# Low-part second products of the first layer one step later, other order at block ends, a third h buffer

## The chip, the cores and the metric

The kernel runs on one core of a Trainium2 chip. A core has five engines that run side by side, each through its own queue in order: TensorE (PE) multiplies, ScalarE (ACT), VectorE (DVE) and GpSimd (POOL) work on tiles, SyncE (SP) issues transfers. The metric is the time of one execution in microseconds (us) as the device counts it; lower is better.

## The reference, cut

```python
X = np.fft.fft(np.fft.fft(x, axis=1), axis=2).real      # x: 2 x 3008 x 256
x = X.reshape(6016, 256)
h = x @ w_in1;  r = maximum(h, 0);  x = (r * r) @ w_out1     # first layer, hidden width 2048
h = x @ w_in2;  out = (h - tanh(h)) @ w_out2                 # second layer
```

## The kernel before

**Precision.** Each operand of a product is split in a high and a low part, and a product is three matmuls: high by high, low by high, high by low. A matmul here takes a stationary block of 128 x 128 weights and streams 376 or 378 columns.

**Staging.** The transform over the sequence is folded into eight blocks of output frequencies (two batches by four classes). The first layer works through (block, f) pairs, f being one of 16 slices of 128 of the hidden layer; STEPS lists them, 128 steps in all. Block 0 runs its first four slices, then block 1 runs whole, then block 0 the rest; from step 32 on the blocks follow one another. The second layer starts when the last block of the first is done.

**One step of the first layer** has five parts, which the loop at L808 calls for different steps in one iteration i:
- `front(i + 2)`, six matmuls (L352, tile w<-uv,wt): the first products, into two PSUM banks. The four banks of `w` hold two steps.
- `back(i)`, twelve matmuls (L517): the second products into four accumulators a00 to a11 (half of the model dimension m, half of the columns s). Eight take gh, the high part of the squared values, and four take gl, the low part.
- `mid(i + 2)`: DVE makes pb (L490) and the two halves of h (L491, L492) from the banks; ACT takes the positive part (L493), squares it into gh (L494) and again into h (L495).
- `late(i + 1)`: POOL (DVE in the first eight slices of block 0) makes gl = h - gh (L504).
- background: conversions, folds and splits of weights for later stages. From step 48 on it is `make_w2` (L543), two of its parts per iteration; they stand on DVE at L227, L229, L231 (conversion from float64), L558 (low part) and L566 to L575 (sums), on ACT at L219, L556 and L573. `tc.issue_after(last_mid[0].ins)` holds them behind the mid of their iteration on DVE.

**Buffers.** gh and gl have three buffers, h has two (L454): DVE may write h of step k at L491 only when POOL has read h of step k - 2 at L504.

**Block ends.** After the last slice of a block (and after slice 3 of block 0) `evac` copies the four accumulators out: ACT those of m = 0, DVE those of m = 1 (L531). The next block's first `back` writes the same four banks; between the two lies one `front`. At three places the transforms of later blocks use the accumulators first (DFT, L822).

**What sets the order.** The engines run in the order in which the scheduler leaves the instructions, which follows the code except where it finds a later one ready sooner. In the last block `restore(f)` loads the second layer's weights over slice f's.

Of the kernel before, what the change touches and what calls it, by code (L numbers as in the profile page):

```python
# [21 lines left out]
# Rows of the sequence that share one folded row n, as (sign, offset): row = offset + sign * n.  # L22
# First two of a half against the last two (their mirror rows).
# [5 lines left out]
# Folded rows n in the order of their partitions, -1 for none: the even ones in the first tile and  # L29
# a half, the odd ones in the rest.  # L30
# [3 lines left out]
# Columns d and 256 - d side by side (0 goes with 128).  # L34
COLS = np.array([list(range(128)), [128] + [256 - d for d in range(1, 128)]])
# Classes of output frequencies k; S - k comes with k.
# [11 lines left out]
# Transforms of later blocks, at the start of a block of the first layer.  # L48
HALF = 4
DFT = {(0, HALF): (2, 3), (3, 0): (4,), (5, 0): (6, 7)}  # L50
# The first block waits with its second half while the weights that it takes are made.
STEPS = [(0, f) for f in range(HALF)] + [(1, f) for f in range(NF)]
STEPS += [(0, f) for f in range(HALF, NF)] + [(blk, f) for blk in range(2, NBLK) for f in range(NF)]
# The steps that make the weights of the first layer.
# [4 lines left out]
def x_layout(x):  # L59
    """Per row tile, the two terms of the sums that the folds begin with: (sums of pieces 0 and 2,  # L60
    of pieces 1 and 3), each for both halves of the columns. The column 0 goes with 128 in sums of
    its own."""
    out = np.zeros((B, 3, 2, 128, 2, 2, 2, 128), x.dtype)
    used = ROWS >= 0
    for g in range(2):
        r = np.zeros((2, 4, B, 384, 128), x.dtype)
        for s, (sg, of) in enumerate(PIECES[g]):
            rows = (of + sg * ROWS[used]) % S
            for h in range(2):
                r[h, s, :, used] = x[:, rows][:, :, COLS[h]].swapaxes(0, 1)  # L70
        r = r.reshape(2, 4, B, 3, 128, 128)
        for s in range(2):
            for i in range(2):
                for term, h in ((0, i), (1, 1 - i)):
                    out[:, :, term, :, i, s, g] = r[h, s + 2 * term]
                    out[:, :, term, :, i, s, g, 0] = r[(i + s) % 2, s + 2 * term, ..., 0]
    return out.reshape(B, 3, 2, 128, 1024)
# [13 lines left out]
def tables():  # L91
    n = ROWS
    w = np.where(n < 0, 0.0, 1.0)
    w[(n == 0) | (n == NROW - 1)] = 0.5
    res = []
    for c, k in enumerate(KS[:3]):
        a = 2 * np.pi * ((k[None, :] * n[:, None]) % S) / S
        first = np.cos(a) * w[:, None]
        if c < 2:
            second = np.sin(a) * w[:, None]  # L100
        else:
            a2 = 2 * np.pi * ((k[None, :] * (752 - n)[:, None]) % S) / S
            second = np.cos(a2) * w[:, None]
        t = np.concatenate([first.reshape(3, 128, -1), second.reshape(3, 128, -1)])
        if c == 0:
            t[:, :, NROW] = 0.0
        # [row tile, 128, (first hi, first lo, second hi, second lo), N]
        t = np.stack(_split(t)).reshape(2, 2, 3, 128, -1).transpose(2, 3, 1, 0, 4)
        res.append(np.ascontiguousarray(t.reshape(3, 128, 4, -1)))
    return res  # L110
# [28 lines left out]
def spectral_mlps(  # L139
# [25 lines left out]
    def psw():  # L165
        """Two banks; as one tile in the first block."""
# [11 lines left out]
    def ring(name):  # L178
        """A tile of the ring that holds tables and inputs of the second layer."""
# [34 lines left out]
    # float64, as pairs of words, to float32: the exponent's bias is changed by a product in the  # L214
    # words' own reading as float32; what is under float32's range comes out as tiny.
# [5 lines left out]
    def conv(layer, f):  # L221
        """Yields after each part."""
        r = raw.pop((layer, f))
        lo, hi = r[:, :, 0], r[:, :, 1]
        y = main.tile([128, 512], I32, tag="cy", name="cy")
# [14 lines left out]
    def transform_in(f, p):  # L240
        """A slice of w1_in under the transform over the model dimension: rows for the even and
        odd parts."""
# [14 lines left out]
    def clear_middle(f):  # L257
        """The middle frequency's row of the odd part, which only the whole products take."""
# [4 lines left out]
    def middle_load(f):  # L263
        """The middle frequency's row of the odd part as a column, in its two parts."""
# [26 lines left out]
    def fold(b, t):  # L291
        """The folded rows for odd k, split in two, and those for even k. Yields after each step."""
# [38 lines left out]
    def split_even(b, t):  # L331
        """Splits the folded rows for even k, in the place of those for odd k."""
# [24 lines left out]
    def dft_mm(blk):  # L357
        """Folded transform over the sequence for one class of even k: even and odd parts."""
# [19 lines left out]
    def dft_pair(blk, t):  # L378
        """Folded transform over the sequence for the classes of odd k, from row tile t: even and
        odd parts, of even rows and of odd rows. The second class has the difference of the two."""  # L380
# [29 lines left out]
    def dft_evac(blk):  # L410
        """The parts split in two, and the middle frequency's row of the even part in all
        partitions."""
# [8 lines left out]
    def pair_evac(blk):  # L421
        """The same for the classes of odd k. Yields after the first class."""
# [30 lines left out]
    def tiles():  # L453
        h = main.tile([128, 2, NM], F32, tag="h", name="h", bufs=2)  # L454
# [25 lines left out]
    def mid(blk, f):  # L480
        n = NC[BLOCKS[blk][1]]
        p = wps.pop((blk, f))
        h, gh, gl = tiles()
        if blk == 0 and f in WHOLE:
            for s in range(2):
                act.activation(h[:, s, :n], bank(p, s)[:, :n], AF.Relu)
        else:
# [4 lines left out]
            last_mid[0] = dve.tensor_tensor(h[:, 1, :n], pb[:, :n], bank(p, 1)[:, :n], ALU.subtract)  # L492
            act.activation(h[:, :, :n], h[:, :, :n], AF.Relu)  # L493
# [12 lines left out]
    def back(blk, f):  # L506
        n = NC[BLOCKS[blk][1]]
        if f == 0 or blk == 0 and f in FIRST:
            acc[1, blk] = [psa(0), psa(1)]
        w = wt[f]  # L510
        first = f == 0 or blk == 0 and f in FIRST
        last = f == NF - 1 or blk == 0 and f in LAST
        gh, gl = gt.pop((1, blk, f))
        for g, wi in ((gh, 2), (gh, 3), (gl, 2)):
            for m in range(2):
                for s in range(2):
                    pe.matmul(  # L517
                        acc[1, blk][m][s][:, :n],
                        w[:, wi, m * 128:(m + 1) * 128],
                        g[:, s, :n],  # L520
                        start=(first and g is gh and wi == 2),
                        stop=(last and g is gl),
                    )

# [14 lines left out]
    # Pairs of slices in seven products: the blocks of w_in are (slice, half of the model  # L539
    # dimension), those of x are (half of the model dimension, half of the columns).  # L540
    sums, x7 = {}, {}

    def make_w2():  # L543
        """The second layer's weights split in two, and the sums of the blocks of w_in."""
# [3 lines left out]
        for f in range(NF):  # L548
# [15 lines left out]
            y = main.tile([128, 512], F32, tag="cy", name="sums")  # L564
# [14 lines left out]
    def load_sums(j):  # L579
        """Gives the parts of the four sums, hi and lo."""  # L580
# [11 lines left out]
    def make_x7(blk):  # L592
        """The blocks of x that are operands as they are, and the sums, split in two."""
# [28 lines left out]
    def pair(blk, j, back, prev, extra):  # L622
        """The products of a pair, with the last pair's second products between them, and what
        comes after the products. Gives the blocks that are not done."""
# [13 lines left out]
        def block(i, k, c, d=None):  # L638
            """Block (slice, half of the columns) of the product, and what comes after it."""
# [24 lines left out]
        step(p21, 1)  # tanh  # L664
        step(c11, 1)  # add
        step(back, 2)
        step(p12, 1)  # copy
        step(p21, 1)  # sub
        step(c11, 2)  # tanh, sub
# [3 lines left out]
        step(p12)  # gl  # L673
        step(c11, 1)  # copy
        step(p21, 1)  # copy
        step(c11)  # gl
        step(p21)  # gl
# [4 lines left out]
        step(c22, 1)  # add  # L682
        step(back, 3)
        step(c22, 2)  # tanh, sub
        product(p, s4, x["b22"], False)
        step(c12, 2)  # tanh
        step(c22, 1)  # copy
        step(c12, 1)  # sub
        step(back)
        product(z, a[3], x["t4"], False)  # L690
        step(c21, 1)  # add
        step(c22)  # gl
        return c12, c21

    def back_pair(blk, j):
        """Yields after each half of a block."""
# [32 lines left out]
    def weights1(f, p):  # L729
        """Converted values of slice f to the operands of its products."""  # L730
# [9 lines left out]
    # so that ScalarE has its functions before it needs them  # L740
# [58 lines left out]
    # tables of later blocks  # L799
# [8 lines left out]
    for i in range(-2, NS - 2):  # L808
# [11 lines left out]
        # transforms of later blocks, while the accumulators are free  # L820
        if (blk, f) in DFT:
# [10 lines left out]
            look(i + 3)  # L832
        if i >= 0:
            back(blk, f)
        if f == NF - 1 or blk == 0 and f in LAST:
            evac(blk, blk == 0 and f == NF - 1)
        mid(*STEPS[i + 2])
        if i >= -1:
            late(*STEPS[i + 1])
        # weights of later steps  # L840
# [16 lines left out]
        # the rest of the folds and the second layer's weights  # L857
# [10 lines left out]
        if blk == NBLK - 1:  # L868
            restore(f)
# [6 lines left out]
        # tables  # L876
# [4 lines left out]
    # the second layer  # L881
    def back_last():
        for f in (NF - 2, NF - 1):
            back(NBLK - 1, f)
            restore(f)
            if f == NF - 1:
                evac(NBLK - 1)
# [23 lines left out]
def w_layout(w_in, w_out):  # L911
    """Per slice of the hidden layer, rows of w_in and of w_out, as the words of the numbers."""
# [22 lines left out]
```

## Time and profile before

| | us |
|---|---|
| Three runs, median (lowest to highest) | 1032.24 (1032.15 to 1033.52) |
| Profiled execution, span from first to last instruction | 1030.0 |
| PE busy | 970.4 (94%) |
| DVE busy | 806.7 (78%) |
| ACT busy | 731.0 (71%) |
| POOL busy | 245.9 (24%) |

The profile is of one execution and gives its span alone; the median of the runs lies 2.2 us above it, and 2.2 us is taken as what lies around the span. A share is a mean over the whole span. A matmul's end is modelled, and it overlaps the next one, so a busy PE is not yet a PE at its best pace. "Idle before" an instruction is time in which its engine had nothing running, with the event that ended it.

### The profile page before, as it was taken

The numbers are of one execution on the slowest core, as the hardware profiler recorded it, in microseconds if no ns is written. First come the engines' busy times: TensorE is split into PE (matmuls) and PEld (weight loads), VectorE is DVE, ScalarE is ACT, GpSimd is POOL, SyncE is SP. The second block draws the span as 40 slices with busy tenths as digits, with TensorE's granted clock in tenths as the row PEclk, the third lists the DMA queues.
The fourth block names the chain that finished last, engine by engine and source line by source line (L and its number), as shares of the span: only waits on it lengthen the run. The fifth ranks groups of instructions, "written<-read, shape, count | busy, mean of one in ns | idle before, by whom it ended". The sixth has DMA issues, their size and how long they took to land.

```text
span 1030.0 us, 15447 instructions
## 1 busy us (share of the span) xinstructions
PE 970.4 (94%) x5542; PEld 948.3 (92%) x5542; DVE 806.7 (78%) x1483; ACT 731.0 (71%) x1289; POOL 245.9 (24%) x171
## 2 busy tenths in 40 slices
PE   4988898999898899898999999999999999999998
PEld 3877897999888898788999999999999999999998
DVE  6999779657898878989567877968778787876776
ACT  2877767787777867877876766767667676766665
POOL 1145515653445435545530000000000000000000
PEclk9999999999999999999999999999999999999999
DMA  8666140206222313514740000101001010000000
GB/s 306 208 202 159 30 142 21 31 1 252 102 94 101 136 70 121 183 62 151 270 160 1 31 31 1 61 1 53 9 1 61 1 61 1 2 31 1 31 1 31
DMA packets 36332, 82.66 MB, mean 80 GB/s; under 512 B 7328, under 2 KB 21152, under 8 KB 36256
## 3 DMA queue, kind: packets, MB, share of 16 engines
q1 hardware_dynamic: 35280, 79.34, 22.0%
q0 software_dynamic: 976, 2.34, 1.4%
q8 instruction: 43, 0.70, 0.3%
q14 instruction: 33, 0.27, 0.1%
HBM read 55.97 MB, written 25.69 MB: 79 GB/s over the span
## 4 chain that ended last, share of the span: by engine, by line
PE 68%; DVE 11%; POOL 4%; ACT 3%; issue 3%; DMA 0%; POOLq 0%; DVEq 0%; ACTq 0%
PE a L352 28%; PE w L352 28%; PE a L517 12%; POOL gl L504 4%; DVE h L491 2%; DVE h L492 2%; ACT h L495 1%; DVE pb L490 1%; ACT gh L494 1%; DVE val L231 1%; DVE val L229 1%; DVE cy L227 1%; DVE sums L569 1%; DVE sums L571 1%; DVE sums L575 0%
## 5 line engine op out<-in xcount | busy, mean ns | idle before, releaser
L504 POOL TENSOR_TENSOR gl<-h,gh 128x752 fp32r<-128x752 f32 (+1 forms) x120 | 224.2, 1868 | 224.0 <-ACT h L495 174.3
L352 PE MATMUL a<-gh,wt 128*128 128x376 f32 (+1 forms) x1024 | 259.6, 335 | 0.0
L517 PE MATMUL a<-gh,wt 128*128 128x376 f32 (+1 forms) x1024 | 205.4, 340 | 6.4 <-DVE y L531 2.4
L517 PEld LDWEIGHTS a<-gh,wt 128*128 128x128 f32 x1024 | 179.8, 190 | 11.8 <-DVE y L531 4.7
L352 PEld LDWEIGHTS a<-gh,wt 128*128 128x128 f32 x1024 | 184.5, 188 | 0.0
L352 PE MATMUL a<-gl,wt 128*128 128x376 f32 (+1 forms) x512 | 171.8, 335 | 0.0
L352 PE MATMUL w<-x,sums 128*128 128x376 f32 (+1 forms) x768 | 163.4, 334 | 0.0
L493 ACT ACTIVATE h<-h 128x752 f32<-128x752 f32 (+1 forms) x125 | 104.1, 832 | 76.9 <-DVE h L492 74.3
L352 PE MATMUL w<-uv,wt 128*128 128x376 f32 (+1 forms) x777 | 156.9, 337 | 0.7 <-POOL wt L259 0.7
L653 DVE TENSOR_TENSOR gl<-h,gh 128x376 fp32r<-128x376 f32 (+1 forms) x256 | 138.8, 546 | 11.3 <-ACT gh L651 10.6
L651 ACT CAST gh<-h 128x376 fp32r<-128x376 f32 (+1 forms) x256 | 129.3, 507 | 17.1 <-DVE h L649 16.8
L517 PE MATMUL a<-gl,wt 128*128 128x376 f32 (+1 forms) x512 | 113.3, 343 | 27.7 <-POOL gl L504 27.7
L352 PEld LDWEIGHTS w<-uv,wt 128*128 128x128 f32 x777 | 136.8, 190 | 1.2 <-POOL wt L259 1.0
L647 ACT ACTIVATE tanh<-h 128x376 f32<-128x376 f32 (+1 forms) x192 | 99.8, 520 | 52.8 <-DVE h L643 47.5
L649 DVE TENSOR_TENSOR h<-h,tanh 128x376 f32<-128x376 f32 (+1 forms) x192 | 106.6, 555 | 37.6 <-ACT tanh L647 31.3
L352 PEld LDWEIGHTS w<-x,sums 128*128 128x128 f32 x768 | 135.4, 188 | 0.2 <-ACT u L681 0.2
L517 PEld LDWEIGHTS a<-gl,wt 128*128 128x128 f32 x512 | 88.8, 190 | 37.3 <-POOL gl L504 37.0
L494 ACT ACTIVATE gh<-h 128x752 fp32r<-128x752 f32 (+1 forms) x128 | 106.9, 835 | 3.0
L495 ACT ACTIVATE h<-h 128x752 f32<-128x752 f32 (+1 forms) x128 | 106.7, 833 | 3.0
L490 DVE SCALAR_TENSOR_TENSOR pb<-ub,w,w 128x376 f32<-128x376 f32 (+1 forms) x125 | 74.9, 600 | 40.0 <-PE w L352 37.4
L643 DVE TENSOR_TENSOR h<-u,w 128x376 f32<-128x376 f32 (+1 forms) x128 | 69.6, 543 | 39.1 <-ACT u L681 39.1
L491 DVE TENSOR_TENSOR h<-w,pb 128x376 f32<-128x376 f32 (+1 forms) x125 | 68.5, 548 | 40.0 <-POOL gl L504 29.6
(98 smaller groups left out, 1129.7 us busy)
## 6 DMA issues: line engine op xcount, KB each, us to landing
stage<-w SPq DMA_DIRECT2D x32, 512.0 KB, 3.7
tab<-tab SPq DMA_DIRECT2D x12, 752.0 KB, 7.8
w2s<-w SPq DMA_DIRECT2D x16, 512.0 KB, 2.6
wt<-w2s SPq DMA_DIRECT2D x16, 512.0 KB, 3.6
sums<-sums SPq DMA_DIRECT2D x15, 512.0 KB, 3.5
tab<-tab SPq DMA_DIRECT2D x6, 756.0 KB, 5.6
x<-y SPq DMA_DIRECT2D x12, 376.0 KB, 3.1
x2f<-x SPq DMA_DIRECT2D x6, 752.0 KB, 4.6
```

What stands on the lines that cost most here:

```text
L352: pe.matmul(dst, a, r, start=(first and i == 0), stop=(last and i == 3 * len(terms) - 1), **kw)
L490: dve.scalar_tensor_tensor(pb[:, :n], ub[:, :n], w128[:, f:f + 1], bank(p, 0)[:, :n], ALU.mult, ALU.add)
L491: dve.tensor_tensor(h[:, 0, :n], bank(p, 1)[:, :n], pb[:, :n], ALU.add)
L493: act.activation(h[:, :, :n], h[:, :, :n], AF.Relu)
L494: act.activation(gh[:, :, :n], h[:, :, :n], AF.Square)
L495: act.activation(h[:, :, :n], h[:, :, :n], AF.Square)
L504: eng.tensor_tensor(gl[:, :, :n], h[:, :, :n], f32(gh[:, :, :n]), ALU.subtract)
L517: pe.matmul(acc[1, blk][m][s][:, :n], w[:, wi, m * 128:(m + 1) * 128], g[:, s, :n], start=(first and g is gh and wi == 2), stop=(last and ...
L647: act.activation(th, c, AF.Tanh)
L649: dve.tensor_tensor(h, c, th, ALU.subtract)
L651: act.copy(gh, h)
L653: dve.tensor_tensor(gl, h, f32(gh), ALU.subtract)
```

## The change

It makes four edits, all in the first layer.

1. `back(i)` issues the eight matmuls on gh of its own step, and then the four on gl of the step before (kept in the list `low`). The first step of a block has eight matmuls; the last issues its own four as well, sixteen in all. The order inside a group of four is now column half outside, model half inside.
2. h has three buffers. To make room for it, the tile `cy` (and `sums` in `make_w2`) takes the tag "p" with the tile of the fold.
3. `mid` is a generator in two parts. Its DVE part is written ahead of `back` and `evac`, its ACT part behind them.
4. `restore(f)` in the last block waits for the next step's `back`.

```diff
@@ tiles, conv, make_w2
-        h = main.tile([128, 2, NM], F32, tag="h", name="h", bufs=2)
+        h = main.tile([128, 2, NM], F32, tag="h", name="h", bufs=3)
-        y = main.tile([128, 512], I32, tag="cy", name="cy")
+        y = main.tile([128, 512], I32, tag="p", name="cy")
-            y = main.tile([128, 512], F32, tag="cy", name="sums")
+            y = main.tile([128, 512], F32, tag="p", name="sums")
@@ mid
-        if blk == 0 and f in WHOLE:
-            for s in range(2):
-                act.activation(h[:, s, :n], bank(p, s)[:, :n], AF.Relu)
-        else:
+        whole = blk == 0 and f in WHOLE
+        if not whole:
...
             last_mid[0] = dve.tensor_tensor(h[:, 1, :n], pb[:, :n], bank(p, 1)[:, :n], ALU.subtract)
+        yield
+        if whole:
+            for s in range(2):
+                act.activation(h[:, s, :n], bank(p, s)[:, :n], AF.Relu)
+        else:
             act.activation(h[:, :, :n], h[:, :, :n], AF.Relu)
@@ back
+    def second(blk, f, g, parts, first=False, last=False):
+        n = NC[BLOCKS[blk][1]]
+        for k, wi in enumerate(parts):
+            for s in range(2):
+                for m in range(2):
+                    pe.matmul(
+                        acc[1, blk][m][s][:, :n],
+                        wt[f][:, wi, m * 128:(m + 1) * 128],
+                        g[:, s, :n],
+                        start=first and k == 0,
+                        stop=last and k == len(parts) - 1,
+                    )
+
+    def back(blk, f):
+        first = f == 0 or blk == 0 and f in FIRST
+        if first:
+            acc[1, blk] = [psa(0), psa(1)]
+        gh, gl = gt.pop((1, blk, f))
+        second(blk, f, gh, (2, 3), first=first)
+        if not first:
+            second(blk, *low.pop(), (2,))
+        if ends(blk, f):
+            second(blk, f, gl, (2,), last=True)
+        else:
+            low.append((f, gl))
@@ the loop over the steps
+        mids = mid(*STEPS[i + 2])
+        step(mids, 1)
         if i >= 0:
             back(blk, f)
-        if f == NF - 1 or blk == 0 and f in LAST:
+        if i >= 0 and ends(blk, f):
             evac(blk, blk == 0 and f == NF - 1)
-        mid(*STEPS[i + 2])
+        step(mids)
         if i >= -1:
             late(*STEPS[i + 1])
...
         if blk == NBLK - 1:
-            restore(f)
+            if f > 0:
+                restore(f - 1)
```

**PE in an ordinary step**, here in block 4 around slice 14. The accumulator is named first, then the tile that streams and the weights' slice. Before:

```order
L517 MATMUL a10_3021<-gh_3463,wt1_14_990 128x376
L517 MATMUL a11_3022<-gh_3463,wt1_14_990 128x376
L517 MATMUL a00_3019<-gl_3464,wt1_14_990 128x376
L517 MATMUL a01_3020<-gl_3464,wt1_14_990 128x376
L517 MATMUL a10_3021<-gl_3464,wt1_14_990 128x376
L517 MATMUL a11_3022<-gl_3464,wt1_14_990 128x376
L352 MATMUL w0_3554<-uv_2416,wt1_1_272 128x376 x3
L352 MATMUL w1_3555<-uv_2416,wt1_1_272 128x376 x3
L517 MATMUL a00_3019<-gh_3503,wt1_15_1075 128x376
```

After:

```order
L520 MATMUL a01_3027<-gh_3447,wt1_14_986 128x376
L520 MATMUL a11_3029<-gh_3447,wt1_14_986 128x376
L520 MATMUL a00_3026<-gl_3413,wt1_13_935 128x376
L520 MATMUL a10_3028<-gl_3413,wt1_13_935 128x376
L520 MATMUL a01_3027<-gl_3413,wt1_13_935 128x376
L520 MATMUL a11_3029<-gl_3413,wt1_13_935 128x376
L352 MATMUL w0_3550<-uv_2416,wt1_1_272 128x376 x3
L352 MATMUL w1_3551<-uv_2416,wt1_1_272 128x376 x3
L520 MATMUL a00_3026<-gh_3487,wt1_15_1071 128x376
```

Behind the gh matmuls of slice 14 now stand the gl matmuls of slice 13, where those of slice 14 itself stood; the front of two steps ahead follows as it did.

**ACT at the end of block 3**, where y is the copy of the accumulators and `sums` is background work that waits for DVE's L571. Before:

```order
L493 ACTIVATE h_2996<-h_2996 128x2x376
L531 COPY y_2988<-a00_2442 128x376
L531 COPY y_2988<-a01_2443 128x376
L494 ACTIVATE gh_2997<-h_2996 128x2x376
L573 CAST sums_3009<-sums_2965 128x512
L495 ACTIVATE h_2996<-h_2996 128x2x376
```

After:

```order
L498 ACTIVATE h_2972<-h_2972 128x2x376
L593 CAST sums_3009<-sums_2961 128x512
L551 COPY y_2995<-a00_2449 128x376
L551 COPY y_2995<-a01_2450 128x376
L499 ACTIVATE gh_2973<-h_2972 128x2x376
L500 ACTIVATE h_2972<-h_2972 128x2x376
```

The background cast has moved from behind the two copies to in front of them (so also at the end of block 4). On DVE, the rows of mid and of the background from step 32 on stand as before but for a few places where neighbours change places; only h's buffer, which no row shows, is another.

## Rows read from the trace of the kernel before

**Rows 1.** Page, part 1: engine, busy us (share of the span) x instructions

```profile
PE 970.4 (94%) x5542; PEld 948.3 (92%) x5542; DVE 806.7 (78%) x1483; ACT 731.0 (71%) x1289; POOL 245.9 (24%) x171
```

**Rows 2.** Windows: stretch, its length, busy us (x instructions) per engine, clock, DMA

```profile
100.00:125.00 25.00, 21.22 (x115) 20.90 (x116) 17.79 (x29) 17.97 (x25) 15.40 (x15) 0.93 0.25 69
...
200.00:225.00 25.00, 25.00 (x147) 25.00 (x146) 12.92 (x25) 20.17 (x25) 14.66 (x9) 1.00 0.01 1
...
600.00:625.00 25.00, 25.00 (x148) 25.00 (x147) 17.93 (x36) 16.21 (x36) 0.00 (x0) 1.00 0.00 1
```

**Rows 3.** Waits of PE: line waited for, us in total, times, longest

```profile
PE a L517 <- POOL gl L504: 27.7, 28, 2.8
...
PE a L517 <- DVE y L531: 2.4, 3, 1.1
PE a L517 <- ACT y L531: 2.3, 3, 1.2
PE a L352 <- DVE y L531: 2.1, 2, 1.7
PE a L517 <- ACT gh L494: 1.5, 2, 0.8
```

**Rows 4.** Windows: eight steps with background, inside block 4

```profile
317.90:346.07 28.17, 25.66 (x146) 24.73 (x145) 23.32 (x38) 22.15 (x29) 14.95 (x8) 1.00 0.25 94
```

**Rows 5.** Groups of DVE by line, same eight steps: busy, mean ns, idle before

```profile
L491 DVE TENSOR_TENSOR h<-w,pb 128x376 f32<-128x376 f32 x8 | 4.4, 550 | 4.7 <-POOL gl L504 4.1
...
L231 DVE SCALAR_TENSOR_TENSOR val<-stage,val 128x512 int32<-128x512 int32 x3 | 3.4, 1126 | 0.0
L229 DVE SCALAR_TENSOR_TENSOR val<-val,cy 128x512 int32<-128x512 int32 x2 | 2.9, 1441 | 0.1
L227 DVE TENSOR_SCALAR cy<-stage 128x512 int32<-128x512 int32 x2 | 2.2, 1102 | 0.0
L571 DVE TENSOR_TENSOR sums<-val,sums 128x128 f32<-128x128 f32 x1 | 1.8, 1790 | 0.0
L558 DVE TENSOR_TENSOR w<-val,w 128x512 fp32r<-128x512 f32 x2 | 1.4, 685 | 0.0
```

**Rows 6.** Timeline of one such step: start, us, instruction, idle before and what ended it

```profile
338.16 1.80 POOL L504 TENSOR_TENSOR gl<-h,gh 128x752 fp32r<-128x752 f32 x1 [2.94 <-ACT h L495]
...
340.00 0.55 DVE L491 TENSOR_TENSOR h<-w,pb 128x376 f32<-128x376 f32 x1 [1.46 <-POOL gl L504]
...
340.02 0.95 PE L517 MATMUL a<-gl,wt 128*128 128x376 f32 x4 [0.84 <-POOL gl L504]
...
340.61 1.81 POOL L504 TENSOR_TENSOR gl<-h,gh 128x752 fp32r<-128x752 f32 x1 [0.64 <-ACT h L495]
...
340.92 1.78 DVE L227 TENSOR_SCALAR cy<-stage 128x512 int32<-128x512 int32 x1
```

**Rows 7.** Timeline of steps without background

```profile
206.30 0.61 DVE L490 SCALAR_TENSOR_TENSOR pb<-ub,w,w 128x378 f32<-128x378 f32 x1 [1.38 <-PE w L352]
...
209.01 0.84 ACT L494 ACTIVATE gh<-h 128x756 fp32r<-128x756 f32 x1
...
209.73 1.55 PE L517 MATMUL a<-gh,wt 128*128 128x378 f32 x8
...
210.85 1.82 POOL L504 TENSOR_TENSOR gl<-h,gh 128x756 fp32r<-128x756 f32 x1 [1.29 <-ACT h L495]
...
212.84 1.37 PE L517 MATMUL a<-gh,wt 128*128 128x378 f32 x7
```

**Rows 8.** Timeline where block 3 ends and block 4 starts

```profile
295.08 0.83 ACT L531 COPY y<-a 128x376 f32<-128x376 f32 x2
...
296.12 0.29 DVE L571 TENSOR_TENSOR sums<-val,sums 128x128 f32<-128x128 f32 x1
...
296.53 0.62 ACT L573 CAST sums<-sums 128x512 fp32r<-128x512 f32 x1
```

**Rows 9.** Windows: the stretch in which the first weights are made

```profile
50.00:100.00 50.00, 43.10 (x262) 40.51 (x260) 47.27 (x84) 35.60 (x58) 24.61 (x29) 1.00 0.59 171
```

More of the change, by code (lines that the diff above doesn't have):

```diff
@@ L504, in late, with ends @@
         eng.tensor_tensor(gl[:, :, :n], h[:, :, :n], f32(gh[:, :, :n]), ALU.subtract)
-    def back(blk, f):
+    def ends(blk, f):
+        return f == NF - 1 or blk == 0 and f in LAST
+    def second(blk, f, g, parts, first=False, last=False):
         n = NC[BLOCKS[blk][1]]
[L508 to L516, printed above, removed]
+        for k, wi in enumerate(parts):
+            for s in range(2):
+                for m in range(2):
                     pe.matmul(
                         acc[1, blk][m][s][:, :n],
-                        w[:, wi, m * 128:(m + 1) * 128],
+                        wt[f][:, wi, m * 128:(m + 1) * 128],
                         g[:, s, :n],
-                        start=(first and g is gh and wi == 2),
-                        stop=(last and g is gl),
-                    )
+                        start=first and k == 0,
+                        stop=last and k == len(parts) - 1,
+                    )
+    def back(blk, f):
[10 more added lines that the diff above has]
+            low.append((f, gl))
+    low = []
     def evac(blk, add=False):
@@ L884, in back_last @@
             back(NBLK - 1, f)
-            restore(f)
+            restore(f - 1)
             if f == NF - 1:
+                restore(f)
                 evac(NBLK - 1)
```

## The prediction

> **What bounds the kernel now.** The page comes first: PE is busy 94% of the span [rows 1]. There is one weight load for each matmul, 5542 of both, so the new order of m and s inside a group saves no load and adds none. The windows say where the other 6% lie. From 600 to 625 us, in the second layer, PE is busy throughout [rows 2]; nothing can be gained there. In the first layer 200 to 225 us is as full, while its other stretches are not. The waits of PE name the reason: 28 waits of the gl matmuls for POOL, 27.7 us, then waits at block ends for the copies of the accumulators, 6.8 us in three lines, and 1.5 us for gh [rows 3].
>
> The waits name who came last, not what is slow. POOL is not: in eight steps with background it is busy 14.95 of 28.17 us [rows 4]. Look instead at DVE in those eight steps. It is busy for 23.3 us [rows 4] and stands idle for 4.7 us before h at L491, 4.1 of them because POOL still reads the h of two steps before [rows 5]. 23.3 + 4.7 = 28.0 of 28.17 us: DVE has no other idle time, so DVE with its wait for a buffer sets the pace, 28.17 / 8 = 3.52 us a step. The timeline shows one turn: POOL ends gl at 338.16 + 1.80 = 339.96, h starts on DVE at 340.00 after an idle 1.46, and PE's gl matmuls start at 340.02 after an idle 0.84 [rows 6]. Both waited for the same POOL instruction, but only DVE's wait delays the steps that follow.
>
> PE's own pace is read where nothing holds it: from 209.73 to 212.84, one step of 18 matmuls in 3.11 us [rows 7], 0.173 us each. In 28.17 us PE loses 28.17 - 8 x 3.11 = 3.3 us.
>
> **The third h buffer.** With it, h of step k waits for POOL's read of step k - 3, a whole step earlier, and 1.46 us of wait, the longest kind in these steps, is under one step. So the 4.1 us go, and DVE needs 28.17 - 4.1 = 24.1 us for eight steps, 3.01 a step, under PE's 3.11. ACT needs 22.15 / 8 = 2.77 and POOL 14.95 / 8 = 1.87 [rows 4]. PE becomes the bound, with DVE only 0.8 us in eight steps behind it; that margin is what the rivals attack.
>
> **gl one step later.** In the clean stretch gl of a step is ready at 210.85 + 1.82 = 212.67, and its matmuls come behind the eight of gh that start at 212.84, so at 212.84 + 8 x 0.173 = 214.2 [rows 7]: 1.5 us to spare. One step later makes it 4.6 us. gh now has the nearest due time: ready at 209.01 + 0.84 = 209.85 and wanted at 212.84, 3.0 us to spare. So DVE may run late by 3.0 us instead of 1.5 before PE stands still. This is what an uneven background needs: a step's DVE work can exceed 3.11 us as long as the mean does not. By itself it does not lift the pace, since DVE would wait for h as before and the late gl would be late by more each step until it showed again. The gl buffer is held a step longer: it comes free at 214.2 + 0.7 + 3.11 = 218.0, and POOL wants it again at 210.85 + 3 x 3.11 = 220.2 [rows 7], so three gl buffers are enough.
>
> **What goes, on PE's path.** A wait's loss is its idle time and a restart: eight matmuls last 1.55 us [rows 7], so the last one is recorded as 1.55 - 7 x 0.173 = 0.34 long, 0.16 more than the pace, and that part of the gap is counted as busy.
> - gl waits: 27.7 + 28 x 0.16 = 32.2 us.
> - gh waits: 1.5 + 2 x 0.16 = 1.8 us.
> - The clock: from 100 to 125 us its mean is 0.93 of the full 2.4 GHz [rows 2], the first of two such stretches; PE had waited for POOL or for copies ahead of both. 2 x 0.07 x 25 = 3.5 us, which I let go with the waits.
>
> Sum 37.5 us. A cross-check: 64 of the 128 steps carry the second layer's weights, and at 3.3 us for eight they lose 26 us; the other 11 lie in the steps before and after them.
>
> **What stays or comes.**
> - Block ends, 9 of them: the last step's own gl is still used in its step, only four matmuls (0.7 us) later than before. A wait like the 0.84 of rows 6 keeps about 0.2 with its restart, 2 us in all (between 0 and 9 x 0.3).
> - ACT at the ends of blocks 3 and 4: the cast of the sums now stands before the copies and waits for DVE's L571, which ends at 296.4, while the copies ran from 295.08 [rows 8]. The copies then end near 298 instead of 295.9. DVE's own copies were late behind L571 already, so I take 1 us of new wait at each, 2 us (between 0 and 2 x 2). The relu of the step also sits before them and gh behind them; the 3.0 us cover that.
> - The first weights, 50 to 100 us: DVE is busy 47.3 of 50 us [rows 9], so at most 2.7 us can be won there; I take off 0.5 us.
> - mid ahead of evac in the code: nothing, as the rows of DVE stand as before where it matters.
> - The tag "p" for `cy` and `sums`: nothing. The fold of batch 1, which shares it, starts at step 20 and ends by step 48; the conversions end near step 14 and start again at step 48. If they met, each would be one DVE instruction late.
> - restore on SP a step later: nothing. The last two slices are wanted in the eighth pair of a second-layer block, and the transfers queued behind on SP are sums for later pairs. If SP were late, the first pair would wait.
>
> 37.5 - 2 - 2 - 0.5 = 33. The span becomes 1030.0 - 33 = 997, and with 2.2 us around it **999 us**.
>
> **The rule that speaks against it.** DVE and POOL get in each other's way in these rows: L571 takes 1.79 us in one place [rows 5] and 0.29 in another [rows 8], and L227, started at 340.92 under a gl that runs from 340.61 to 342.42, ends at 342.70 [rows 6]. Background that comes behind a running gl waits for its end, while h at L491, which reads a PSUM bank, keeps its 550 ns [rows 5]. The Trainium skill, page "SBUF — State Buffer", section "Who interferes with whom", has this as a rule: whichever of the two issues first holds the shared port pair for its whole instruction and the other fully blocks. By that rule a faster PE packs the same gl time into shorter steps, and DVE would be blocked more often; the trace agrees with the lock and can't show the new overlap.
>
> **Rivals.**
> A. *The lock takes half of the wait's place.* Now the lock costs, over the 0.69 of L558: L227 2 x 0.41, L229 2 x 0.75, L231 3 x 0.44, and L571 1.5, together 5.1 us in eight steps [rows 5, 8]. gl is 1.87 of 3.52 us now and of 3.11 after, from 53% to 60%. If 2.5 us are added, DVE needs (24.1 + 2.5) / 8 = 3.32 a step, the 64 steps gain 13 us instead of 26, and the time is 999 + 13 = 1012.
> B. *The lock grows past the wait, slower.* If each of the eight gl blocks a background instruction for 1.5 us, as with L571, the lock is 12 us and DVE needs (24.1 - 5.1 + 12) / 8 = 3.88 a step, 0.36 over now. 64 steps lose 23 us, the rest gains 7, and the time is 1032 + 16 = 1048. It decides from 5.1 + 4.1 = 9.2 us of lock in eight steps. Against it: background starts right behind mid, and most of it fits before the next gl when DVE is not late.
> C. *Nothing happens.* h waits for something else that comes just as late, such as the PSUM banks or ACT, and the pace stays: 1032. Against it: ACT at 2.77 a step, and DVE in clean steps waits for PE, 1.38 us before pb [rows 7].
> D. *More.* The waits for copies, 6.8 us, shrink as well, since half the accumulators are done earlier by the new order: 999 - 9 = 990.
>
> **How the numbers follow.** The forecast has 0.70, from 995 (all of the 37.5) to 1005 (upper ends of the block-end costs, 2.7 more, and a quarter of A's growth, 3). A has 0.14, D 0.06, C 0.05, B 0.05. The range reaches from D to A, 989 to 1013, and leaves out about 0.1 to 0.2. Faster by over 0.2% (2.1 us, about what a measurement of this kernel can tell from no change): forecast, A and D, 0.90. Within it: C, 0.05. Slower: B, 0.05.
>
> **What would show it.** In the changed profile: h at L491 no longer waits for POOL; PE's gl waits fall from 27.7 us to under 4; steps with background take 3.1 to 3.2 us, DVE idle before pb on PE rather than before h; PE from 250 to 475 us near full. If gl waits are gone but PE waits for gh with DVE never idle, A or B is right: then the mean of L227, L229 and L571 has grown. If the step is still 3.5 us and DVE waits elsewhere, C. Second-layer windows must stay as they are.

## The result and the profile after

| | before | after |
|---|---|---|
| median of four runs (lowest to highest), us | 1032.38 (1032.15 to 1033.52) | 1006.93 (1006.82 to 1008.9) |
| ratio, 95% interval | | 0.9757 (0.9744 to 0.9771) |
| span of the profiled execution, us | 1030.0 | 1005.1 |
| granted clock of the span | 0.997 | 0.995 |

The change gains 25 us. The forecast was 999, so 33 us: the direction was right, the time lies inside the range of 989 to 1013 but outside the forecast's own 995 to 1005, and 8 us of the gain did not come. The page of after, part 1 (engine, busy us and its share of the span), answers to [rows 1]:

```profile
PE 963.3 (96%) x5542; PEld 950.5 (95%) x5542; DVE 787.4 (78%) x1483; ACT 726.7 (72%) x1289; POOL 251.6 (25%) x171
```

The waits of PE after (line waited for, us in total, times, longest), beside [rows 3]. L509, L499, L520 and L551 are the L504, L494, L517 and L531 of before:

```profile
...
PE w L247 <- DVE val L231: 7.7, 5, 4.0
PE a L520 <- ACT gh L499: 5.8, 6, 1.5
PE a L520 <- ACT y L551: 5.0, 3, 2.9
PE a L520 <- DVE y L551: 4.2, 3, 2.0
...
PE a L520 <- POOL gl L509: 0.5, 1, 0.5
```

The line that the change aimed at is gone: 28 gl waits of 27.7 us became one of 0.5. In its place gh waits grew from 1.5 to 5.8 us, waits for copies from 6.8 to 9.2, and those for the weights' values (L231) from 5.7 to 7.7.

What a step with background looks like now, on DVE and PE inside block 4 (start, us, instruction, idle before); it answers to [rows 6]:

```profile
299.50 0.61 DVE L490 SCALAR_TENSOR_TENSOR pb<-ub,w,w 128x376 f32<-128x376 f32 x1 [0.77 <-PE w L352]
...
299.81 1.55 PE L520 MATMUL a<-gh,wt 128*128 128x376 f32 x8
300.24 0.55 DVE L491 TENSOR_TENSOR h<-w,pb 128x376 f32<-128x376 f32 x1
...
302.60 0.61 DVE L490 SCALAR_TENSOR_TENSOR pb<-ub,w,w 128x376 f32<-128x376 f32 x1 [0.76 <-PE w L352]
```

h at L491 starts with no wait, and DVE now waits ahead of pb, for PE: the step is 302.60 - 299.50 = 3.10 us. Windows of after (stretch, length, busy us per engine with instructions, clock, DMA) show where PE is full and where it is not:

```profile
75.00:100.00 25.00, 20.96 (x122) 20.66 (x121) 24.86 (x45) 15.89 (x26) 12.17 (x14) 0.93 0.49 121
100.00:125.00 25.00, 21.69 (x117) 20.79 (x116) 15.33 (x29) 17.61 (x24) 16.62 (x15) 0.93 0.23 61
300.00:325.00 25.00, 25.00 (x147) 25.00 (x146) 20.52 (x38) 22.04 (x30) 16.03 (x9) 1.00 0.29 108
...
450.00:475.00 25.00, 23.04 (x125) 22.56 (x124) 19.30 (x34) 20.32 (x28) 14.37 (x8) 0.93 0.70 251
```

From 300 to 325 us PE is busy throughout, with 147 matmuls in 25 us, as the kernel before has from 200 to 225 us [rows 2]. From 75 to 125 us, and at the end of a block, it still loses time, and the clock falls in three stretches, not two.

### The profile page after: what moved, and what is told of

It is laid out like the page before. It is cut to its first block, busy times and chain, and to the rows that moved or that the text cites. A ratio compares the mean times of both kernels' runs of the same rounds, so it can differ in the third digit from the quotient of the medians.

```text
span 1005.1 us, 15446 instructions
## 1 busy us (share of the span) xinstructions
PE 963.3 (96%) x5542; PEld 950.5 (95%) x5542; DVE 787.4 (78%) x1483; ACT 726.7 (72%) x1289; POOL 251.6 (25%) x171
## 4 chain that ended last, share of the span: by engine, by line
PE 80%; DVE 12%; issue 3%; ACT 2%; DMA 2%; POOL 0%; SPq 0%; DVEq 0%; POOLq 0%; ACTq 0%
PE w L352 32%; PE a L352 29%; PE a L520 18%; DVE pb L490 2%; DVE h L491 2%; DVE h L492 1%; DMA p<-x 1%; DVE val L231 1%; DVE val L229 1%; DMA stage<-w 1%; ACT gh L499 1%; DVE p L321 1%; DVE wt L238 1%; PE w L247 1%; DMA mcol<-wt 0%
## 5 line engine op out<-in xcount | busy, mean ns | idle before, releaser
L509 POOL TENSOR_TENSOR gl<-h,gh 128x752 fp32r<-128x752 f32 (+1 forms) x120 | 230.0, 1925 | 195.2 <-ACT h L500 135.3
L520 PE MATMUL a<-gh,wt 128*128 128x376 f32 (+1 forms) x1024 | 204.4, 341 | 15.1 <-ACT gh L499 5.8
L520 PEld LDWEIGHTS a<-gh,wt 128*128 128x128 f32 x1024 | 179.4, 191 | 21.0 <-ACT gh L499 8.7
L352 PE MATMUL a<-gl,wt 128*128 128x376 f32 (+1 forms) x512 | 171.7, 335 | 0.0
L490 DVE SCALAR_TENSOR_TENSOR pb<-ub,w,w 128x376 f32<-128x376 f32 (+1 forms) x125 | 75.1, 601 | 56.5 <-PE w L352 48.6
L520 PE MATMUL a<-gl,wt 128*128 128x376 f32 (+1 forms) x512 | 109.1, 336 | 0.5 <-POOL gl L509 0.5
L499 ACT ACTIVATE gh<-h 128x752 fp32r<-128x752 f32 (+1 forms) x128 | 106.9, 835 | 2.9
L352 PEld LDWEIGHTS a<-gl,wt 128*128 128x128 f32 x512 | 96.4, 188 | 0.4 <-DVE gl L673 0.3
L520 PEld LDWEIGHTS a<-gl,wt 128*128 128x128 f32 x512 | 90.8, 190 | 0.8 <-POOL gl L509 0.8
```

What stands on the lines that cost most here:

```text
L352: pe.matmul(dst, a, r, start=(first and i == 0), stop=(last and i == 3 * len(terms) - 1), **kw)
L490: dve.scalar_tensor_tensor(pb[:, :n], ub[:, :n], w128[:, f:f + 1], bank(p, 0)[:, :n], ALU.mult, ALU.add)
L499: act.activation(gh[:, :, :n], h[:, :, :n], AF.Square)
L509: eng.tensor_tensor(gl[:, :, :n], h[:, :, :n], f32(gh[:, :, :n]), ALU.subtract)
L520: pe.matmul(acc[1, blk][m][s][:, :n], wt[f][:, wi, m * 128:(m + 1) * 128], g[:, s, :n], start=first and k == 0, stop=last and k == len(par ...
```

## Experiments

Runs of one group were made on one chip, with the kernel before beside them, and chips differ by some us. So they are compared by ratio to before. The changed kernel stood at 0.9757 in the first comparison and at 0.9794 (0.9781 to 0.9808) in e5_after_again below. The two intervals don't overlap, so a difference of 0.4% between groups shows nothing.

**Which edit sets the pace.** The third h buffer alone, on the kernel before (`cy` and `sums` take the tag "p" for room), and the changed kernel without it:

```diff
@@ before, e1_h3_only
-        h = main.tile([128, 2, NM], F32, tag="h", name="h", bufs=2)
+        h = main.tile([128, 2, NM], F32, tag="h", name="h", bufs=3)
@@ after, e2_order_only
-        h = main.tile([128, 2, NM], F32, tag="h", name="h", bufs=3)
+        h = main.tile([128, 2, NM], F32, tag="h", name="h", bufs=2)
```

> The kernel before with the third h buffer alone (and the shared tag that makes room for it). Theory, the buffer sets the pace: DVE's 29.6 us of waits for POOL before h are gone, and the 64 steps with the second layer's weights fall from 3.52 us to between 3.11 and 3.3, since gl still has only 1.5 us to spare; PE keeps some gl waits, 5 to 15 us instead of 27.7. Time 1007 to 1020. Rival, the later gl is what matters: PE's gl waits stay near 27 us and the time is 1028 to 1033.

> The changed kernel with two h buffers again: later gl matmuls and the new code order alone. Theory, the buffer sets the pace: DVE waits for POOL before h as in the kernel before (25 to 35 us), the pace of the 64 steps stays near 3.5 us, PE's waits move from gl to gh or to the first products, time 1026 to 1036. Rival, the later gl is what matters: 1007 to 1015.

e1_h3_only: 0.9856 (0.9825 to 0.9887). Of its gl waits one line is left:

```profile
PE a L517 <- POOL gl L504: 14.4, 15, 2.7
```

e2_order_only: 0.9995 (0.9979 to 1.0011), no gain. Its waits of PE and of DVE:

```profile
PE a L520 <- ACT gh L499: 14.8, 15, 2.5
...
PE a L520 <- POOL gl L509: 2.6, 5, 0.6
```

```profile
DVE h L491 <- POOL gl L509: 34.5, 30, 2.9
```

So the buffer sets the pace, as predicted: without it DVE waits for POOL in thirty places, and most of PE's wait only gets another name, gh for gl; waits for copies grow as well, from 6.8 to 12.7 us. The clock takes a part in the 0.9995: the profiled execution of e2_order_only had 0.987 (before 0.997), and its one run at 0.997 took 1027.97 us, so the order alone may gain some 3 us. With the buffer, 14.4 us of gl waits stay in the old order, and the late gl removes them: from 0.9856 to 0.9757 or 0.9794. That step holds the code order of `mid` and the later `restore` too. `restore` had no run of its own; from the gh matmuls of the first layer's last step to the end the changed kernel takes 501.8 us, the kernel before 500.9.

**The place of mid.** The changed kernel with mid whole behind `back` and `evac`:

```diff
@@ e4_mid_as_before
-        mids = mid(*STEPS[i + 2])
-        step(mids, 1)
...
-        step(mids)
+        step(mid(*STEPS[i + 2]))
```

> The changed kernel with mid as one piece behind back and the copies again, as in the kernel before: undoes the order at block ends alone. Theory, that edit buys nothing or costs the ends a little: 1003 to 1008. Rival, it is part of the gain: over 1010, with DVE's mid held behind the copies at nine ends, 0.5 to 1.5 us each.

0.9801 (0.9779 to 0.9823), 1009.92 us, between its two expectations. The changed kernel did not run beside it: from 0.9794 in the next group it does not differ, from 0.9757 in the first comparison it does. Its waits of PE for gh and for copies, 5.5 and 10.3 us, are near the 5.3 and 9.2 of e5_after_again. So no worth of this edit shows, as the prediction priced it, but a difference of some us is not ruled out.

**Block ends.** First the background is left out of the steps that end a block (it is done one step later), in the changed kernel:

```diff
@@ e3_ends_quiet
-        if i >= 8:
+        if i >= 8 and not ends(blk, f):
```

> The changed kernel without background work in the steps that end a block (it runs one step later instead, nothing is left out). Theory, the background that the scheduler put ahead of the accumulators' copies costs the changed kernel its block ends: the waits of PE for copies fall from 9.2 us to about 5, those at the ends of blocks 3, 5 and 6 (1.8, 2.1, 2.0 us) to under 0.7 each, time 1001 to 1004. Rival, the ends wait for the copies anyway: 1006 to 1008.

0.9802 (0.9775 to 0.983): the expectation failed. The wait at the end of block 3 halved (0.88 us for 1.75), those of blocks 5 and 6 did not shrink (2.48 us at 401, 1.99 at 458). Leaving the step's background out did not help there, because DVE ran work for the second layer (x2f, below) ahead of the copies instead: L634 for 1.87 us at 398 and L636 for 1.71 us at 456. Next the copies were put first on both engines, beside the changed kernel as it is:

```diff
@@ e6_copies_first: at a block's end
-        step(mids, 1)
+        if i < 0 or not ends(blk, f):
+            step(mids, 1)
...
             evac(blk, blk == 0 and f == NF - 1)
+            with tc.issue_after(last_y[0].ins), tc.issue_after(last_y[1].ins):
+                step(mids)
```

> The changed kernel as it stands, as the base of this group of runs. Every theory: 0.973 to 0.978 of the kernel before, PE's waits at block ends for the copies y about 9 us, for gh about 6 us, two falls of the clock around 90 and 112 us and one near 457 us.

> The changed kernel, but in a step that ends a block the copies of the accumulators come first on DVE and ACT, ahead of the next step's pb, h, relu and gh, and the background behind those. Theory (the y waits at the block ends come from where the copies stand in the two queues): two copies take 1.0 us and PE has six matmuls, 1.2 us, ahead of its first gh matmul, so the y waits fall from 9 us to under 2 and the clock fall near 457 us goes; 6 to 9 us less than the changed kernel, 998 to 1001. Rival (the copies are late because DVE is late as a whole at block ends, or gh turns up late in their place): y or gh waits stay at 7 us or more together at these places, and the time stays within 2 us of the changed kernel's.

e5_after_again: 0.9794 (0.9781 to 0.9808), a little outside what was expected, at clock 0.988. e6_copies_first: 0.9756 (0.9743 to 0.9769), 1005.83 us for 1009.07. Neither expectation held: 3 us are gained where 6 to 9 or at most 2 stood. The theory held for DVE (PE's waits for its copies 4.2 us in e5_after_again, 0.2 here) and failed for ACT (5.0 and 6.2), and gh waits rose from 5.3 to 6.9. In e6_copies_first, where block 6 ends (lines one higher):

```profile
450.90 2.13 DVE L635 TENSOR_TENSOR x2f<-x2f 128x376 f32<-128x376 f32 x1
453.07 0.55 DVE L637 TENSOR_TENSOR x2f<-x2f 128x376 f32<-128x376 f32 x1
453.54 1.00 DVE L552 COPY y<-a 128x378 f32<-128x378 f32 x2
453.65 0.82 ACT L624 CAST x<-x2f 128x752 fp32r<-128x752 f32 x1 [3.10 <-DVE x2f L637]
454.38 0.84 ACT L552 COPY y<-a 128x378 f32<-128x378 f32 x2
...
454.90 1.33 PE L521 MATMUL a<-gh,wt 128*128 128x376 f32 x6 [3.24 <-ACT y L552]
```

ACT stands idle for 3.10 us ahead of a cast of x2f, and the copies stand behind that cast. The cast waits for DVE, whose L635 takes 2.13 us beside 0.55 for L637, which has the same shape. x2f is an input of the second layer: its code stands in the last block or behind it, and nothing kept the scheduler from issuing it up to two blocks early. The edge that holds the background behind mid holds its DVE instructions only.

**One abs at 105 us.** In the changed kernel, ACT and PE between 105 and 107 us:

```profile
105.19 0.66 ACT L219 ACTIVATE val<-stage 128x512 f32<-128x512 f32 x1 [3.32 <-DMA stage<-w]
105.76 0.81 ACT L499 ACTIVATE gh<-h 128x752 fp32r<-128x752 f32 x1
```

```profile
106.63 0.61 PE L520 MATMUL a<-gh,wt 128*128 128x376 f32 x2 [1.49 <-ACT gh L499]
```

PE waits for the next gh as well, 1.52 us at 110.47. L219 is the first abs of the second layer's weights, which the code issues in step 48. ACT takes it near step 14 and waits there for its transfer; gh comes behind. One edge moves it:

```diff
@@ e7_abs_behind_gh: make_w2
+            if f == 0:
+                with tc.issue_after(last_mid[1].ins):   # the gh of the step
+                    conv_abs(2, f)
```

> The changed kernel, with one edge more: the first abs of the second layer's weights (L219, stage of w2) comes behind the gh of step 48 on ACT and not at 105 us, where it waits 3.3 us for its transfer with a gh behind it. Theory (this one instruction makes the two gh waits at 106 and 110 us, and the fall of the clock behind them): the 3.0 us of gh waits there go and the fall at 112 us with its 1.7 us, 3 to 5 us less than the changed kernel. Rival (ACT or DVE is late there anyway, or the weights of slice 14 are): waits of PE between 104 and 112 us stay at 2.5 us or more and the time within 1.5 us of the changed kernel's.

0.9741 (0.9724 to 0.9758), 1003.06 us for 1009.07: 5 to 6 us by the medians. Two of its five runs took 1007.2 and 1007.7 us, at a clock of 0.990; the profile is of one of them, and its steps 0 to 31 take 4.5 us less than those of e5_after_again (134.7 for 139.2). Its window answers to the second of the windows above:

```profile
100.00:125.00 25.00, 25.00 (x150) 25.00 (x149) 18.76 (x35) 20.47 (x29) 16.29 (x15) 1.00 0.26 74
```

150 matmuls for 117 (115 at a clock of 0.86 in e5_after_again), at full clock: both gh waits and the fall of the clock went with one instruction. gh waits in all fell from 5.3 us to 3.5.

**How much DVE has to spare.** One more addition on DVE in each of the steps 48 to 111, its result used by nothing, of 128x512 and then of 128x256:

```diff
@@ e8_dve_load (e10_dve_half takes 256 of the 512 columns)
+                    if i < 112:
+                        z = wtab[:, :, :, :].rearrange("p a b n -> p (a b n)")
+                        v = f32(wt[0]).rearrange("p a n -> p (a n)")
+                        dve.tensor_tensor(z, v[:, :512], v[:, 512:], ALU.add)
```

> The changed kernel with one DVE addition of 128x512 more in each of steps 48 to 111, its result used by nothing (0.69 us unblocked by the row of L558 of the same size, so 5.5 us in eight steps). By the margin in the prediction, 0.8 us in eight steps, DVE becomes the bound: (5.5 - 0.8) / 8 x 64 = 38 us more, about 1045. If DVE now has the 4.5 to 7.5 us free in eight steps that the windows of the changed kernel's profile from 300 to 350 us leave, the sum is 0 to 1 us in eight steps: 0 to 8 us more, 1007 to 1015.

> As the run with one more DVE addition in each of steps 48 to 111, but 128x256, 0.41 us by the row of L319 of the same size. Theory (DVE on time meets the lock less: 20.0 us busy of 25 from 300 to 400 us, 2.49 a step, so 2.90 with the addition, under PE's 3.11): 0 to 6 us more than the changed kernel, 0.979 to 0.985 of the kernel before. Rival (the price is that of a late DVE, 2.92 a step as in the eight steps of before, 3.33 with the addition): DVE late in most steps, 0.22 x 64 = 14 us more, 0.991 to 0.995.

e8_dve_load: 1.0215 (1.0202 to 1.0229), over e5_after_again by 0.0421 x 1030.7 = 43 us. e10_dve_half: 1.008 (1.0039 to 1.0122), over it by 29 us, with single runs from 1030.5 to 1045.0; neither of its two expectations held. Windows of e10_dve_half:

```profile
300.00:325.00 25.00, 24.89 (x145) 24.59 (x143) 24.09 (x40) 17.62 (x24) 13.00 (x7) 1.00 0.27 93
325.00:350.00 25.00, 22.64 (x130) 22.32 (x130) 23.93 (x45) 21.69 (x29) 15.77 (x8) 1.00 0.25 88
350.00:375.00 25.00, 24.27 (x130) 24.01 (x131) 16.93 (x31) 17.25 (x26) 8.01 (x5) 0.93 0.40 143
```

The addition took 0.883 us and 0.604 us on the mean of 300 to 400 us, so 64 of them are 56.5 and 38.7 us of DVE. DVE as a whole was busy for 67.2 and 39.0 us more than in e5_after_again (857.7 and 829.5 for 790.5): the longer addition also makes the rest of DVE's work slower. 43 and 29 us reached the end, but the clock differs too: 0.994 and 0.979 for 0.988, some 6 us less and 9 us more. Without that, as an estimate, the prices are 49 and 20 us, so 18 and 19 us of DVE's work were hidden, about 2.3 us in eight steps. That is three times the prediction's margin of 0.8, and half of DVE's idle time, 4.9 us in eight steps (80.2 us busy from 300 to 400 us in the changed kernel). That e8_dve_load came out near its first expectation, 38 us, is luck: that sum had too small a load and too small a margin.

Why the other half is no reserve was not tested. The rows show that DVE is full in some stretches (24.09, 23.93) and idle in the next (16.93), and a PE that is busy throughout has little with which to win a lost step back.

**All of it together.** The copies first, and every ACT instruction of the background behind the gh of its step; then the split of x2f held in the last block too, two parts a step, and last one part a step:

```diff
@@ e9_both_orders: on top of e6_copies_first
-            with tc.issue_after(last_mid[0].ins):
+            with tc.issue_after(last_mid[0].ins), tc.issue_after(last_mid[1].ins):
@@ e11_x7_in_place: on top of it (e12_x7_spread: step(x7_next, 1))
-                step(x7_next, 2)
+                with tc.issue_after(last_mid[0].ins), tc.issue_after(last_mid[1].ins):
+                    step(x7_next, 2)
```

> The kernel of the run with the copies first, and every ACT instruction of the background also behind the gh of its step, not only the first abs. Theory (what is left of the y and gh waits comes from casts of the background that stand ahead of copies or gh on ACT and wait for a DVE instruction or a transfer): y waits of PE fall from 6.4 us to under 2.5, gh waits from 6.9 to under 2.5, the clock falls at 111 and 456 us go; 0.966 to 0.970 of the kernel before. Rival (a cast that comes later makes the DVE instruction behind it wait, and pb or h behind that): new waits of DVE for casts of several us, 0.974 to 0.978.

> The kernel of the run with both orders, and the split of the first input of the second layer (x2f, b11, x20 to x22) kept behind the mid of its own steps, in the last block, instead of at the ends of blocks 5 and 6 where DVE and ACT take it early. Theory (these instructions, up to 2 us each under a gl, hold the copies up at 394 and 448 us): the two y waits there, 1.8 and 2.1 us, go with their two falls of the clock; 4 to 7 us less than the run with both orders, 0.963 to 0.966 of the kernel before. Rival (the same work, some 10 us of DVE, costs as much in the last block, where DVE has the second layer's weights too): gh or gl waits of 4 us or more between 450 and 500 us and 0.968 to 0.974.

> As the run with the split in its place, but one part of it a step instead of two, so that it lies over twelve steps. Theory: the same y waits go, and no step of the last block has more than 2 us of it: 0.962 to 0.966. Rival (DVE has no reserve in the last block in any step): gh waits there of 4 us or more, 0.968 to 0.974.

| | us (before beside it) | ratio, 95% interval | waits of PE for y; for gh, us |
|---|---|---|---|
| e5_after_again | 1009.07 (1030.70) | 0.9794 (0.9781 to 0.9808) | 9.2; 5.3 |
| e9_both_orders | 999.29 (1030.85) | 0.9694 (0.9678 to 0.9710) | 5.7; 1.5 |
| e11_x7_in_place | 998.18 (1031.36) | 0.9679 (0.9666 to 0.9693) | 1.6; 3.5 |
| e12_x7_spread | 995.11 (1031.36) | 0.9649 (0.9636 to 0.9662) | 1.7; 1.9 |

e9_both_orders met its ratio and its gh waits (6.9 us in e6_copies_first, 1.5 here), but not its y waits: it kept 4.8 us of waits for ACT's copies, most of them at 394 and 448 us, where x2f still stood, with the falls of the clock behind them. e11_x7_in_place removed those and paid for half of it in the last block, where PE now waits for gh, gl and h; its ratio is at the rival's edge and can't be told from that of e9_both_orders. Spread over twelve steps the same work fits. The waits of PE in e12_x7_spread (lines one higher):

```profile
...
PE w L247 <- DVE val L231: 7.2, 5, 3.7
PE a L352 <- DVE xo L315: 2.8, 1, 2.8
PE a L521 <- ACT gh L500: 1.9, 7, 0.4
...
PE a L521 <- ACT y L552: 0.9, 1, 0.9
...
PE a L521 <- POOL gl L510: 0.5, 1, 0.5
```

```profile
450.00:475.00 25.00, 25.00 (x147) 25.00 (x146) 15.77 (x28) 21.94 (x29) 17.69 (x10) 1.00 0.73 243
```

It beats both kernels: 36 us under before and, by the ratios 0.9794 and 0.9757, 15 or 11 us under the change. 0.9649 x 1032.4 is 996 us, inside the 995 to 1005 of the forecast. The longest wait left in these steps is PE's for L231 near 88 us (3.7 us). In e7_abs_behind_gh, where it is 4.06 us, DVE's two instructions ahead of that L231 read:

```profile
82.83 2.82 DVE L227 TENSOR_SCALAR cy<-stage 128x512 int32<-128x512 int32 x1
...
85.68 2.29 DVE L229 SCALAR_TENSOR_TENSOR val<-val,cy 128x512 int32<-128x512 int32 x1
```

The shortest L229 of this run takes 0.68 us, and two gl of POOL run beside the pair, from 83.22 and from 85.66 us. That this is the lock of the prediction was not tried by an experiment, and the start times alone don't explain it: L227 starts 0.39 us ahead of the first gl.

## Why the prediction was right, and by how much it was wrong

In the order of the prediction's steps, us of change in the time, a restart counted at 0.16 per wait:

| term | forecast | measured |
|---|---|---|
| gl waits, with 2 us left at block ends | -30.2 | 27 waits and 27.2 us less: -31.5 |
| gh waits | -1.8 | 4 waits and 4.3 us more: +4.9 |
| copies at block ends | +2 | 2 waits fewer, 2.4 us more: +2.1 |
| the clock | -3.5 | one more stretch of 0.93: +1.7 |
| first weights | +0.5 | 1 wait fewer, 2.0 us more: +1.8 |
| sum | -33.0 | -21.0, against -24.9 of span |

The measured terms leave 4 us of gain without a name, 5 with three short waits for weights and h that the table leaves out and that are 1.0 us longer after. They don't lie in gaps: span less busy time less all listed waits is 3.9 us before and 3.7 after. They lie in what counts as PE's busy time, which fell by 7.1 us [rows 1]; fewer restarts are 3.8 of that, and the clock worked against it with 1.7 us. What the rest is stays open.

Where the time went shows when steps are counted in the two timelines, eight gh matmuls each. Step 32 starts at 178.5 us in both kernels: the first 32 steps gave nothing. Steps 48 to 111 take 238.2 us before and 215.4 after, 22.8 us less where the cross-check has 26. The rest gave 2 us, where the sum wants 7. So most of the miss lies outside the steps that the argument is about.

- **What bounds the kernel, and the third buffer: right.** Without the buffer no gain shows (0.9995); with it h no longer waits, and PE is busy throughout from 300 to 400 us. One reading is off and changes nothing: not only 200 to 225 us was full before, but 225 to 250 us as well (25.00 us busy).
- **gl a step later: right.** Alone it gains little or nothing; behind the buffer it takes 13.9 of the remaining 14.4 us of gl waits. The 2 us kept for gl at block ends were 0.5.
- **The gh waits: the step that failed.** It took them as gone, because gh is ready 3.0 us before it is wanted. That is true in clean steps [rows 7], but it holds only while nothing stands ahead of gh on ACT. In the changed kernel a single abs with a wait of 3.32 us did, and e7_abs_behind_gh shows that it made the two waits (3.0 of the 5.8 us) and the fall of the clock behind them. The other gh waits were not traced one by one; the edge on all of ACT's background takes them from 6.9 us to 1.5 (e6_copies_first, e9_both_orders).
- **The clock: failed with it.** "I let go with the waits" was right only if no new waits came. Up to 178 us the old gl waits were replaced by others (L231 at 88 us, 4.04 us; gh at 106 and 110; ACT's copies at 178, 2.88 us), and the clock fell behind those at 88 and 110. Those copies start at 178.0 us in both kernels, behind the next step's work on ACT, so what PE had won by then it waited for there. Why the wait for L231 grew stays open.
- **Block ends: the size was right by luck.** The cast of the sums did move ahead of the copies (1.75 us at block 3), but at the end of block 4 a wait of 1.68 us went instead of 1 us coming. The new waits are those at 178 us and at the ends of blocks 5 and 6. There DVE's copies stand behind the next step's mid and x2f in both kernels (L605 before, L625 after, 0.93 us), and in the changed one behind a sum of the background as well: L589 takes 1.30 us at 400.92 and 0.96 us at 454.46, just ahead of the copies, where the kernel before has the copies first (at 479.47, L569 at 480.39). The prediction had priced such changes of neighbours at nothing, and x2f it had not seen. e6_copies_first takes the waits for DVE's copies away, e11_x7_in_place those that x2f still made.
- **DVE's margin of 0.8 us in eight steps: too small.** The loads put it at some 2.3 us. It was worked out with the lock of before kept, and the lock shrank instead: with the same 1483 instructions DVE is busy for 787.4 us, 806.7 before [rows 1]. DVE's groups from 300 to 400 us, before and then after (count | busy, mean ns), with seven conversions in both (x7 at L229):

```profile
L229 DVE SCALAR_TENSOR_TENSOR val<-val,cy 128x512 int32<-128x512 int32 x7 | 8.0, 1136 | 0.2
L231 DVE SCALAR_TENSOR_TENSOR val<-stage,val 128x512 int32<-128x512 int32 x6 | 6.8, 1132 | 0.0
...
L569 DVE TENSOR_TENSOR sums<-sums,val 128x128 f32<-128x128 f32 x3 | 4.1, 1373 | 0.0
```

```profile
L231 DVE SCALAR_TENSOR_TENSOR val<-stage,val 128x512 int32<-128x512 int32 x7 | 6.7, 955 | 0.0
L229 DVE SCALAR_TENSOR_TENSOR val<-val,cy 128x512 int32<-128x512 int32 x7 | 4.8, 692 | 0.2
...
L589 DVE TENSOR_TENSOR sums<-sums,val 128x128 f32<-128x128 f32 x3 | 0.9, 285 | 0.0
```

All background rows of that stretch together fell from 39.9 us of DVE for 42 instructions to 33.1 for 46. Single rows move both ways: L229 is back at 900 ns in e5_after_again, and L227 and L578 (L558 before) rose, from 1203 and 685 ns to 1251 and 836. Rivals A and B, which let the lock grow, are out. So is C, since the step is 3.10 us, and D, since the waits for copies grew. That the time lies between the forecast and A is not A's doing. B's cause is real, though: with DVE made late again, in e8_dve_load, L231 is back at this:

```profile
L231 DVE SCALAR_TENSOR_TENSOR val<-stage,val 128x512 int32<-128x512 int32 x6 | 10.6, 1758 | 0.0
```

Counted in the timelines, of the 104 background instructions that make the second layer's weights 43 start under a running gl before, 40 in the changed kernel and 54 in e8_dve_load. What shrank in the changed kernel is less their number than the time that they then take: L227's ten last 1.62 us on the mean before and 1.24 after. The prediction had it the other way, since gl fills more of a shorter step.

The rule of the Trainium skill, page "SBUF — State Buffer", section "Who interferes with whom", is that the first to issue holds the shared ports for its whole instruction and the other blocks. These rows agree with it; L227 at 82.83 us in e7_abs_behind_gh, which starts ahead of its gl and is long all the same, does not follow from it alone.

## What to carry to other kernels

When a buffer is what an engine waits for, one more of it is worth its memory, and a reordering that moves the consumer alone is not: try each by itself. After the first bound is lifted, look for what stands ahead of the next instruction that is due on each in-order queue: an edge that holds background behind the main work must name an instruction on every engine that the background runs on. Idle time of an engine in a window is only in part a reserve, here about half; add work to it and measure.

## What the runs showed of the hardware

Two executions of the same changed kernel have the same stall at the end of block 3 (1.75 and 1.76 us), and the clock fell behind it in one of them only. The window of the first, then of e5_after_again:

```profile
275.00:300.00 25.00, 23.25 (x136) 22.85 (x135) 21.28 (x37) 22.07 (x31) 15.47 (x8) 1.00 0.35 127
```

```profile
275.00:300.00 25.00, 23.24 (x126) 22.85 (x125) 21.13 (x35) 21.55 (x31) 15.46 (x8) 0.93 0.38 136
```

0.07 x 25 = 1.7 us, as much again as the stall itself. So a stall's price carries a part that differs between runs. The number of stalls alone does not tell the clock: e12_x7_spread ran at 0.998 with waits of at most 0.9 us at its block ends, the kernel before at 0.997 with its 28 gl waits, the changed kernel at 0.995 and 0.988.
